# A new hand-over order and later, wider warm-up matmuls in an attention and feed-forward kernel

## The chip, the cores and the metric

The kernel runs on one core of a Trainium2 chip. Its five engines each take their instructions in order from a queue of their own: PE multiplies matrices, ACT and DVE work element by element, POOL and SP mostly issue transfers here. [...] The metric is device time in microseconds (us) of one execution; lower is better.

## The reference

Linear attention, whose result is the input of a two-layer network without biases and with an ELU between the layers.

```
q, k, v: (8, 8, 576, 64)                     # batch, head, row, channel; float32
q_s = exp(q - max) / sum over channels
k_s = exp(k - max) / sum over rows
kv  = einsum('bhsd,bhse->bhde', k_s, v)
att = einsum('bhsd,bhde->bhse', q_s, kv)
x   = att.transpose(0, 2, 1, 3).reshape(4608, 512)
h   = x @ w_in                               # (512, 2048)
g   = where(h > 0, h, exp(min(h, 0)) - 1)
out = g @ w_out                              # (2048, 512)
```

## The kernel before

The attention is cut into 16 units (one of 8 batches and four of its eight heads, all 576 rows). For a unit, ACT takes the exponential of the queries (tile QR) and keys (KR), DVE sums the queries (ZQ), inverts the sums and multiplies (QS); PE transposes QS (`tp`) into PSUM, ACT and DVE copy it to qsT; PE multiplies keys and values (`kv_mm`, 36 small matmuls), DVE scales the result into MBLK (`m`); PE multiplies qsT by MBLK (`ao_mm`) and ACT and DVE copy the rows to XT (`xt`). From the fifth unit on, the transpose is done by a transfer (`turn`, tile QT). The network runs over nine blocks of 512 rows: `hg_mm` makes 256 hidden columns at a time (eight matmuls of 512 columns with W1), the `hg` that follows turns them by exponential and comparison into GT on ACT and DVE, and `out_mm` multiplies GT by W2.

`Sched` records every operation with what it reads and writes. Nothing is scheduled at run time: the table ORDER lists, for each engine, the numbers of the operations in the order in which they are issued; numbers go by the order of `add`. The method `order` walks these lists with modelled durations to find a common sequence, `fill` adds warm-up matmuls on PE that compute nothing that is used, and `emit` puts in the semaphore waits. Numbers used below: 0 clears the identity ID; 1 (POOL) writes its diagonal; 25, 26, 27 are the sum, reciprocal and product of unit 0's queries, 37, 38, 39 those of unit 1; 30 and 28 are unit 0's transposes, 43 and 45 unit 1's; 32 and 50 are the key-value products; 47 and 54 the attention products; 49 and 46 are DVE's copies of XT (unit 0) and qsT (unit 1); 67 and 68 the first W1 matmuls.

The first loads (queries, keys, values of units 0 and 1) are issued by SP, in that order; POOL issues W1 once ID and the keys of unit 0 are there, then W2's four slices and the loads of units 2 and 3. The GT buffer of block 1 shares its memory with small buffers of the start, among them OSBX0 to OSBX3, from which the rows of block 0 are stored; DVE may write GT of block 1 there only after those stores have landed. In SP's list 161, 162 are the two stores of OSBX0, 164, 165 those of OSBX1, 167, 168 of OSBX2 and 170, 171 of OSBX3; 185 and 209 are transposes by transfer; 187, 190, 199, 200, 210, 216 are loads.

In `fill` of before, a run of warm-ups is put wherever PE is modelled idle for long enough, one for each 80 ns, 128 columns wide, and waits only for the identity:

```
idle = o.start - free - 150
count = int(idle / 80)
...
p.deps = {d: "raw" for d in self.spare_after}
```

Of the kernel before, what the change touches and what calls it, by code (L numbers as in the profile page):

```python
# [21 lines left out]
ISSUE = {"sp": 550, "act": 550, "gp": 740}  # L22
ORDER = {
    "pe": (
        "30 28 32 43 45 47 50 67 54 68 70 71 69 72 82 86 93 115 103 90 129 128 137 136 131 139 107 "
        "130 138 109 151 152 150 126 134 149 132 156 157 158 140 173 146 153 159 172 174 175 233 238 "
        "237 239 192 243 249 245 244 251 250 201 255 257 256 203 263 262 212 268 261 267 269 313 309 "
        "321 317 350 220 325 333 329 280 391 334 282 338 342 291 412 346 351 299 399 404 395 417 362 "
        "400 364 408 425 430 373 413 421 438 426 381 479 434 439 487 450 500 492 483 505 488 452 513 "
        "518 461 496 469 501 526 509 564 514 572 522 538 585 527 540 568 577 573 598 581 586 590 594 "  # L30
        "603 611 549 607 636 599 556 657 640 612 662 644 649 653 645 670 622 666 624 683 688 658 679 "
        "632 675 671 634 696 709 684 692 701 714 697 705 722 727 735 718 710 740 731 748 723 744 761 "
        "736 766 757 753 749 770 787 762 774 779 775 783 788 792 793 805 797 801 809 "),
    "act": (
        "3 22 33 23 24 31 29 34 35 48 44 55 73 76 77 79 83 84 87 94 95 97 104 91 92 116 117 119 98 "
        "108 120 127 135 133 163 160 179 147 166 154 169 205 176 230 231 188 234 180 240 241 191 246 "
        "215 252 253 202 258 204 211 264 213 265 273 270 214 218 310 322 314 217 284 318 221 279 326 "
        "294 355 281 330 296 335 283 290 392 343 297 292 339 293 347 366 352 376 300 405 361 396 378 "
        "363 401 409 365 372 418 375 443 414 454 379 422 374 431 427 382 464 435 449 480 440 451 466 "
        "493 467 484 531 489 453 460 463 506 519 462 497 470 502 542 510 515 565 537 523 539 554 551 "  # L40
        "528 569 578 574 541 552 616 582 591 587 595 548 555 550 608 637 600 626 557 604 641 613 650 "
        "654 621 646 623 663 667 689 631 625 659 680 633 676 672 685 693 715 702 698 635 706 719 728 "
        "711 732 741 724 745 737 767 758 750 771 754 763 776 780 784 789 794 798 806 802 810 812 "),
    "dve": (
        "2 4 5 0 6 7 25 26 37 27 38 39 40 41 42 36 46 49 51 52 53 56 74 75 78 80 81 85 88 89 96 100 "
        "105 106 101 102 122 118 110 111 112 123 124 141 142 143 148 155 182 183 184 177 178 232 206 "
        "235 236 193 194 207 195 196 197 242 208 247 198 248 254 259 260 266 274 275 271 272 276 311 "
        "312 285 319 222 223 286 320 224 225 226 227 287 327 328 356 331 332 357 336 337 358 344 345 "
        "348 349 367 353 368 354 301 369 302 303 304 305 306 397 398 402 403 410 411 444 415 416 445 "
        "446 423 424 428 429 383 384 455 385 386 387 388 436 456 457 437 441 442 485 490 486 532 491 "  # L50
        "498 499 533 471 503 472 534 473 474 504 511 543 544 512 475 476 516 517 524 525 545 529 530 "
        "570 571 575 576 583 584 596 597 617 588 618 589 609 610 601 558 602 619 642 643 559 627 560 "
        "561 562 614 615 628 629 563 655 656 647 648 668 669 660 661 673 674 681 682 686 687 694 695 "
        "707 699 708 700 720 721 712 713 733 734 725 726 746 747 738 739 759 760 751 752 772 764 765 "
        "773 777 778 785 786 "),
    "gp": (
        "1 14 15 16 17 18 19 20 21 57 59 58 63 60 61 62 64 66 99 65 113 125 144 121 114 145 181 186 "
        "189 "),
    "sp": (
        "8 9 10 11 12 13 170 187 161 164 171 185 165 190 200 168 162 199 209 210 216 167 219 277 278 "  # L60
        "229 228 323 315 288 295 316 289 324 298 341 359 308 360 377 307 340 393 370 371 406 394 420 "
        "380 407 419 447 433 390 465 482 432 458 448 389 494 481 495 459 468 478 507 520 535 477 567 "
        "508 521 536 553 566 546 580 547 579 620 605 638 606 593 592 630 651 652 639 677 665 690 664 "
        "678 703 716 717 691 730 704 729 756 768 769 742 755 743 782 781 790 791 795 796 799 800 807 "
        "808 803 804 811 "),
}


# [14 lines left out]
class Sched:  # L83
# [2 lines left out]
    ENG = ("pe", "act", "dve", "gp", "sp")  # L86
    OVER = {"pe": 163, "act": 105, "dve": 82, "gp": 110}
    LAND = 350
    SPIN_FROM = 9400.0
    FIRST = {"sp": 2050, "act": 2050, "gp": 2700}  # L90
    DMA_RATE = 385.0

# [67 lines left out]

    def fill(self, seq):

        out, free, done = [], self.SPIN_FROM, False
        for o in seq:
            if o.eng == "pe" and not done:
                idle = o.start - free - 150
                count = int(idle / 80)
                if count > 1 and all(d.end < free for d in self.spare_after):
                    p = Op("pe", count * 57, self.spare(count), 0)
                    p.start, p.end = free, free + p.dur  # L170
                    p.deps = {d: "raw" for d in self.spare_after}
                    out.append(p)
                free = o.end
                done = o is self.spare_until
            out.append(o)
        return out

    def emit(self, seq):
# [61 lines left out]
class Gen:  # L240
# [394 lines left out]
    def program(self):  # L635
# [28 lines left out]
        for o in S.ops:  # L664
# [1 line left out]
                o.late = False  # L666
        S.spare_after = [self.ident]
        S.spare = lambda count: lambda e: [e.matmul(
            self.PS[0][:, 0:128], self.ID[:, :], self.ID[:, :], start=True, stop=True)
            for _ in range(count)][-1]  # L670

        self.load_w2(0, -29)
# [87 lines left out]
        key = 0  # L760
# [101 lines left out]
```

The softmax here doesn't subtract the row's maximum and nothing guards it: scores larger than these inputs give would overflow.

## Time and profile before

| | us |
|---|---|
| median of 4 runs | 300.98 (300.61 to 301.87) |
| profiled execution, its own time | 300.78 |
| its span, first to last instruction | 299.0 |
| PE busy | 286.7 |
| DVE busy | 189.5 |
| ACT busy | 182.0 |

The span is what the profile's rows lie in; the execution's time has 1.8 us around it. PE's matmuls are pipelined and the end of each is modelled, so the pace of a group is better read from its start to the start of the next group than from its duration. A bracket at the end of a timeline row gives the engine's idle time before it and what ended that. Engine PEld is PE's loading of weights, which runs beside its matmuls. In the rows of windows the columns are the stretch, its length, then busy time and count of PE, PEld, DVE, ACT and POOL, the granted clock, the share of the transfer engines and their GB/s.

### The profile page before, as it was taken

The page shows a single profiled execution, that of the slowest core. Times are in us where ns is not written, and L with a number is a line of the kernel's source. Part 1 is how long each engine was busy: PE and PEld are TensorE (multiplying, and loading weights), DVE is VectorE, ACT ScalarE, POOL GpSimd, SP SyncE. Part 2 cuts the span into 40 slices and gives each one's busy share as a digit, 9 for nine tenths or more (in the row PEclk, how much of TensorE's full clock was granted, in tenths as well). Part 3 has the DMA queues.
Part 4 walks back from the last instruction along what each step waited for, and adds up shares of the span by engine and source line. Part 5 has one row for each costly group of instructions (what it writes and reads, how often), then busy time and mean ns, then how long its engine had stood idle before and what let it go on. Part 6 is the DMA issues. An engine that isn't in the chain of part 4 may idle for free.

```text
span 299.0 us, 4448 instructions
## 1 busy us (share of the span) xinstructions
PE 286.7 (96%) x1865; PEld 236.1 (79%) x1865; DVE 189.5 (63%) x244; ACT 182.0 (61%) x212; POOL 21.7 (7%) x33
## 2 busy tenths in 40 slices
PE   1699999999999999999999999999999999999995
PEld 1578877687888888888888888888888888888885
DVE  3958935985898685894568855588427256655500
ACT  5768848998977967867755766534462423432411
POOL 0860244100000000000000000000000000000000
PEclk9999999999999999999999999999999999999999
DMA  7999998995497896389546226041312302004214
GB/s 262 395 396 391 389 389 262 280 285 198 120 277 227 125 350 187 73 261 275 166 116 165 89 78 172 2 100 37 85 37 50 72 0 53 0 0 107 64 41 105
DMA packets 35443, 49.96 MB, mean 167 GB/s; under 512 B 16352, under 2 KB 16608, under 8 KB 35424
## 3 DMA queue, kind: packets, MB, share of 16 engines
q1 hardware_dynamic: 29840, 34.15, 41.7%
q0 software_dynamic: 5504, 15.47, 16.2%
q8 instruction: 14, 0.23, 0.3%
q10 hardware_dynamic: 80, 0.07, 0.1%
q14 instruction: 5, 0.04, 0.0%
HBM read 36.70 MB, written 9.44 MB: 154 GB/s over the span
## 4 chain that ended last, share of the span: by engine, by line
PE 92%; DMA 4%; ACT 1%; DVE 0%; SPq 0%; POOL 0%; issue 0%
PE PS L588 44%; PE PS L543 43%; PE PS L487 3%; DMA KR<-in_k_dram 2%; DMA W<-in_moe_w_in_dram 2%; PE PS L456 2%; ACT ESB L559 1%; DVE GT L572 0%; ACT ESB L570 0%; PE PS L403 0%; SPq L315 0%; POOL W L332 0%; ACT OSB L598 0%
## 5 line engine op out<-in xcount | busy, mean ns | idle before, releaser
L588 PE MATMUL PS<-W,GT 128*128 128x512 f32 (+1 forms) x592 | 141.4, 386 | 0.4 <-DVE GT L578 0.4
L543 PE MATMUL PS<-XT,W 128*128 128x512 f32 x576 | 140.3, 391 | 0.2
L543 PEld LDWEIGHTS PS<-XT,W 128*128 128x128 f32 x576 | 107.2, 188 | 23.2 <-DVE XT L512 0.5
L588 PEld LDWEIGHTS PS<-W,GT 128*128 128x128 f32 x592 | 107.7, 188 | 22.1 <-DVE GT L578 0.8
L559 ACT ACTIVATE ESB<-PS 128x1024 f32<-128x1024 f32 x72 | 73.8, 1027 | 65.5 <-PE PS L543 65.3
L576 DVE TENSOR_SCALAR ESB<-ESB 128x1024 f32<-128x1024 f32 x64 | 44.2, 692 | 66.6 <-ACT ESB L559 65.9
L578 DVE TENSOR_TENSOR GT<-ESB,PS 128x1024 fp32r<-128x1024 f32 x64 | 77.7, 1217 | 1.8
L620 ACT ACTIVATE OSB<-PS 128x512 f32<-128x512 f32 x31 | 18.2, 597 | 30.6 <-PE PS L588 30.6
L372 DVE TENSOR_REDUCE ZQ<-QR 128x18 f32<-128x1152 f32 x16 | 21.5, 1343 | 7.3 <-ACT QR L352 7.2
L509 ACT ACTIVATE XT<-PS 128x512 fp32r<-128x512 f32 (+6 forms) x32 | 19.5, 609 | 8.1 <-PE PS L487 7.6
L380 DVE TENSOR_TENSOR QS<-QR,RZQ 128x1152 f16<-128x1152 f32 x16 | 21.6, 1353 | 0.3
L352 ACT ACTIVATE QR<-QR 128x1152 f32<-128x1152 f32 x16 | 18.6, 1165 | 2.8 <-DMA QR<-in_q_dram 2.8
L356 ACT ACTIVATE KR<-KR 128x1152 bf16<-128x1152 f32 x16 | 18.4, 1160 | 2.3 <-DMA KR<-in_k_dram 2.3
L487 PE MATMUL PS<-qsT,MBLK 128*128 128x320 f32 (+5 forms) x64 | 14.4, 311 | 0.0
L487 PEld LDWEIGHTS PS<-qsT,MBLK 128*128 128x128 f32 x64 | 12.0, 194 | 2.6 <-DVE MBLK L469 0.2
L431 ACT ACTIVATE qsT<-QT 128x1152 fp32r<-128x1152 f16 x12 | 13.9, 1162 | 0.0
L365 ACT ACTIVATE VB<-VR 128x1152 bf16<-128x1152 f32 (+1 forms) x12 | 13.5, 1125 | 0.7 <-DMA VR<-in_v_dram 0.7
L572 DVE SCALAR_TENSOR_TENSOR GT<-PS,ESB 128x1024 fp32r<-128x1024 f32 x8 | 9.8, 1221 | 4.5 <-ACT ESB L570 4.4
L403 PE MATMUL PS<-ID,QS 128*128 128x128 f16 x36 | 3.7, 266 | 6.8 <-DVE QS L380 6.8
L469 DVE TENSOR_TENSOR MBLK<-PS,RZK 64x128 fp32r<-64x128 f32 x32 | 9.2, 288 | 0.9
L403 PEld LDWEIGHTS PS<-ID,QS 128*128 128x128 f16 x36 | 2.9, 122 | 7.4 <-DVE QS L380 7.0
L570 ACT ACTIVATE ESB<-ESB 128x1024 f32<-128x1024 f32 x8 | 8.5, 1060 | 0.2
(29 smaller groups left out, 60.0 us busy)
## 6 DMA issues: line engine op xcount, KB each, us to landing
out_dram<-OSB SPq DMA_DIRECT2D x62, 128.0 KB, 2.4
QR<-in_q_dram SPq DMA_DIRECT2D x12, 576.0 KB, 4.7
KR<-in_k_dram SPq DMA_DIRECT2D x12, 576.0 KB, 5.9
VR<-in_v_dram SPq DMA_DIRECT2D x12, 576.0 KB, 5.4
W<-in_moe_w_out_dram POOLq DMA_DIRECT2D x4, 1024.0 KB, 18.2
QR<-in_q_dram POOLq DMA_DIRECT2D x4, 576.0 KB, 11.1
KR<-in_k_dram POOLq DMA_DIRECT2D x4, 576.0 KB, 11.2
VR<-in_v_dram POOLq DMA_DIRECT2D x4, 576.0 KB, 8.1
```

The costliest lines, as they stand in the source:

```text
L352: S.add("act", t_act(1152, False), lambda e: e.activation(flat(q), flat(q), AF.Exp), key - 3, X=[f"qR{i}"], follow=self.table)
L356: S.add("act", t_act(1152, False), lambda e: e.activation(ek[:, :, :, :].rearrange("p h c d -> p (h c d)"), flat(k), AF.Exp), key - 2, X=[ ...
L372: S.add("dve", t_dve(1152), lambda e: e.tensor_reduce(self.ZQ[i][:, :, :].rearrange("p h c -> p (h c)"), q[:, :, :, :].rearrange("p h c d ...
L380: S.add("dve", t_dve(1152), lambda e: e.tensor_tensor(qso, q[:, :, :, :], rz, ALU.mult), key - 3, R=[f"qR{i}", f"RZQ{i}"], W=[f"QS{self.al ...
L487: last = e.matmul(P[:, y:y + n_], M[:, f, :], T[:, c0:c1, f * 64:f * 64 + 64], start=True, stop=True)
L509: S.add("act", t_act((h1 - h0) * n_, True), lambda e, dst=dst, src=src: e.activation(dst, src, AF.Copy), key, W=W, X=X)
L543: last = e.matmul(P[:, t * 512:(t + 1) * 512], self.W1[:, kc, tt * 128:(tt + 1) * 128], self.XT[:, kc, rc:rc + BLK], start=(kc == 0), stop ...
L559: S.add("act", t_act(1024, True), lambda e: e.activation(esb[:, :], P[:, :], AF.Exp), key, W=[f"E{i}"], X=banks)
L576: S.add("dve", t_dve(1024, 2), lambda e: e.tensor_scalar(esb[:, :], esb[:, :], 1.0, -1.0, ALU.min, ALU.add), key, X=[f"E{i}"])
L578: S.add("dve", t_dve(1024), lambda e: e.tensor_tensor(gt, esb[:, :], P[:, :], ALU.max), key, R=[f"E{i}"], W=gw, X=banks)
L588: last = e.matmul(dst, GT[:, jj, ts * 128:(ts + 1) * 128], self.W2[:, jj, c0:c1], start=(jj == 0), stop=(jj == 15))
L620: S.add("act", t_act(512, True), lambda e: e.activation(osb[:, :], src, AF.Copy), key, W=[f"O{i}0", f"O{i}1"], X=[f"b{bk}"])
```

## The change

Three things are changed. All five lists of ORDER are new. In `fill`, a run of warm-ups may start from 7.9 us of the modelled time on, waits also for the last ACT or DVE operation that is modelled to end before it, and is counted with 430 ns for one in the first run and 260 ns in the later ones; the test that the identity is modelled ready is gone. A warm-up is now 512 columns wide: the identity repeated four times as the moving operand. The built program has runs of 3, 3 and 5 warm-ups in place of 12, 3 and 6: 3 ahead of operation 30, 3 ahead of 32 and 5 ahead of 47.

```diff
 ORDER = {
     "pe": (
-        "30 28 32 43 45 47 50 67 54 68 70 71 69 72 82 86 93 115 103 90 129 128 137 136 131 139 107 "
-        "130 138 109 151 152 150 126 134 149 132 156 157 158 140 173 146 153 159 172 174 175 233 238 "
-        "237 239 192 243 249 245 244 251 250 201 255 257 256 203 263 262 212 268 261 267 269 313 309 "
+        "30 28 32 47 43 45 50 68 54 67 70 71 69 72 82 86 93 103 90 115 129 128 107 137 136 130 109 "
+        "131 138 150 126 139 152 132 159 157 149 156 134 140 151 146 153 173 175 158 172 174 233 239 "
+        "237 192 243 238 244 245 251 250 249 256 201 257 203 255 263 262 212 261 267 268 269 313 321 "
...
     "act": (
-        "3 22 33 23 24 31 29 34 35 48 44 55 73 76 77 79 83 84 87 94 95 97 104 91 92 116 117 119 98 "
+        "3 22 33 23 24 29 34 31 35 48 44 55 73 76 77 79 83 84 87 97 94 95 104 91 98 92 116 108 119 "
...
     "dve": (
-        "2 4 5 0 6 7 25 26 37 27 38 39 40 41 42 36 46 49 51 52 53 56 74 75 78 80 81 85 88 89 96 100 "
+        "4 5 2 6 7 25 26 0 27 37 38 39 40 41 42 36 49 46 51 52 53 56 74 75 78 80 81 85 88 89 100 96 "
...
     "gp": (
-        "1 14 15 16 17 18 19 20 21 57 59 58 63 60 61 62 64 66 99 65 113 125 144 121 114 145 181 186 "
+        "1 14 15 16 17 18 19 20 21 59 57 60 58 61 63 62 66 64 65 113 99 125 114 121 144 145 181 186 "
         "189 "),
     "sp": (
-        "8 9 10 11 12 13 170 187 161 164 171 185 165 190 200 168 162 199 209 210 216 167 219 277 278 "
+        "8 9 10 11 12 13 185 187 164 162 190 167 161 200 199 171 209 216 165 168 210 170 277 229 278 "
...
-    SPIN_FROM = 9400.0
+    SPIN_FROM = 7900.0
...
     def fill(self, seq):
 
-        out, free, done = [], self.SPIN_FROM, False
+        free, done, spares = self.SPIN_FROM, False, []
+        timed = [o for o in seq if o.eng in ("act", "dve") and not o.dma]
         for o in seq:
             if o.eng == "pe" and not done:
-                idle = o.start - free - 150
-                count = int(idle / 80)
-                if count > 1 and all(d.end < free for d in self.spare_after):
-                    p = Op("pe", count * 57, self.spare(count), 0)
+                count = int((o.start - free - 150) / (430 if free == self.SPIN_FROM else 260))
+                if count > 0:
+                    p = Op("pe", count * 220, self.spare(count), 0)
                     p.start, p.end = free, free + p.dur
                     p.deps = {d: "raw" for d in self.spare_after}
-                    out.append(p)
+                    near = [d for d in timed if d.end + self.hop(d, p) <= free]
+                    p.deps[max(near, key=lambda d: d.end)] = "raw"
+                    spares.append((o, p))
                 free = o.end
                 done = o is self.spare_until
-            out.append(o)
+        out = []
+        for o in seq:
+            out += [p for q, p in spares if q is o] + [o]
         return out
...
         S.spare = lambda count: lambda e: [e.matmul(
-            self.PS[0][:, 0:128], self.ID[:, :], self.ID[:, :], start=True, stop=True)
+            self.PS[0][:, 0:512], self.ID[:, :], self.ID[:, :].unsqueeze(1).broadcast_to([128, 4, 128]),
+            start=True, stop=True)
             for _ in range(count)][-1]
```

## The prediction

> **What bounds the kernel now.** I read the page's busy shares and chain of waits, then the first 18 us of the timeline, then PE's gaps in the body, then SP's queue.
>
> ```profile
> PE 286.7 (96%) x1865; PEld 236.1 (79%) x1865; DVE 189.5 (63%) x244; ACT 182.0 (61%) x212; POOL 21.7 (7%) x33
> PE 92%; DMA 4%; ACT 1%; DVE 0%; SPq 0%; POOL 0%; issue 0%
> ```
>
> PE is the bound: its matmuls make 92% of the chain that ends last, so any gap in PE after the stream has begun lengthens the run by itself. Before that, the head counts. The timeline (start, duration):
>
> ```profile
> 1.54 0.28 POOL L293 TENSOR_SCALAR_AFFINE_SELECT ID<-ID 128x128 f16<-128x128 f16 x1 [1.10 <-DVE VB L302]
> ...
> 1.88 1.46 PE L668 MATMUL PS<-ID 128*128 128x128 f16 x12 [1.88 <-POOL ID L293]
> ...
> 7.30 0.27 DVE L376 RECIPROCAL RZQ<-ZQ 128x18 f32<-128x18 f32 x1
> 7.48 1.29 DVE L372 TENSOR_REDUCE ZQ<-QR 128x18 f32<-128x1152 f32 x1
> ...
> 8.69 1.34 DVE L380 TENSOR_TENSOR QS<-QR,RZQ 128x1152 f16<-128x1152 f32 x1
> ...
> 10.09 1.14 PE L403 MATMUL PS<-ID,QS 128*128 128x128 f16 x9 [6.75 <-DVE QS L380]
> ...
> 11.17 0.71 PE L456 MATMUL PS<-VB,KR 64*64 64x65 bf16 x36
> ...
> 13.03 1.20 PE L487 MATMUL PS<-qsT,MBLK 128*128 128x512 f32 x2
> ...
> 14.03 0.63 PE L668 MATMUL PS<-ID 128*128 128x128 f16 x6
> 14.59 0.48 PE L456 MATMUL PS<-VB,KR 64*64 64x65 bf16 x36
> 15.21 1.17 PE L543 MATMUL PS<-XT,W 128*128 128x512 f32 x4
> ```
>
> The twelve old warm-up matmuls run at 1.88, then PE idles 6.75 us. The granted-clock column says 1.00 everywhere, but the pace does not: nine transposes take 1.07 us from their start at 10.09 to the next group's (0.119 each), and 0.49 us at 36.39; 36 key-value products (L456) take 0.71 us at 11.17 and 0.48 at 14.59. So PE runs at about half speed until a point between 14.03 and 14.59, 3.9 to 4.5 us after it became steadily busy. The first feed-forward matmuls stand at 15.21 just behind the first W1 slices, whose transfer ends at 15.12 in the chain:
>
> ```profile
> 9.20 5.92 DMA W<-in_moe_w_in_dram
> ```
>
> **The change, part by part.** The sum is made on the profiled execution, 300.78 us with a span of 299.0. The median is 300.98, 0.20 above it.
>
> *Identity.* In DVE's new order the memset of ID stands behind unit 0's sum and reciprocal (7.30 + 0.27 = 7.57), no longer at the start. Before, PE began 0.6 us after that memset ended (1.19 + 0.11 = 1.30, then 1.88), so the first new warm-up starts at about 8.2. It names an ACT operation, unit 1's query exponential (ended at 7.38), but that is not what it waits for longest. Behind it in PE's queue stand unit 0's transposes. W1's first transfer waits for ID too, and for unit 0's keys (8.16 before): cost nothing, covered by the six loads ahead of it in the transfer engines; uncovered, some 0.1 us.
>
> *Unit 0's query product.* It moves ahead of unit 1's sum on DVE (7.48, 1.29), so it ends near 9.0, not 10.03.
>
> *Warm-ups, 3 + 3 + 5 of 512 columns.* At half speed one costs four 128-wide ones: 12 took 1.46 with the tail of the last, so 0.105 to 0.119 each, 0.42 to 0.48; I take 0.42. At full speed 0.227 (60 in 13.7). PE then runs: 8.2, three to 9.47 (transposes were ready at 9.1); transposes 1.07 to 10.54; three to 11.81; key-value product 0.65 (11.16 to 11.81 before) to 12.46. If the clock again takes 3.9 to 4.5 us from the start of steady work, it is full at 12.1 to 12.7. Five warm-ups at full speed end at 13.6. The attention product (L487) could have started at about 13.1, when ACT's second copy of qsT, now behind unit 1's key exponential, is done; the warm-ups hold it 0.5 us.
>
> *XT and the first bank.* L487 at full speed reaches its copy in 0.65 us (16.22 to 16.88), so at 14.25. DVE now does the XT copy before unit 1's qsT copy (both 0.69), and PE's first W1 matmuls go to the bank that the second copy frees: 14.25 + 1.40 + 0.07 = 15.7, against 15.21. Then eight matmuls and unit 1's product, ten at 0.227, reach the second W1 half at 17.97 against 17.62: +0.3. Ends: -0.1 if the clock is early (15.21 + 2.27 = 17.48; W1's landing forbids more); +1.9 if it is never full before (five at 0.42 to 14.56, L487's 1.25 to its copy, 1.47, 2.27: 19.5).
>
> [...]
>
> *The new order in the body.* The largest gaps of PE:
>
> ```profile
> 50.05 4.70 PE L543 MATMUL PS<-XT,W 128*128 128x512 f32 x20
> ...
> 55.13 1.21 PE L588 MATMUL PS<-W,GT 128*128 128x512 f32 x4 [0.38 <-DVE GT L578]
> ...
> 56.42 2.11 PE L543 MATMUL PS<-XT,W 128*128 128x512 f32 x8
> ```
> ```profile
> 52.00:56.00 4.00, 3.62 (x17) 2.61 (x15) 3.77 (x4) 3.90 (x4) 1.15 (x1) 1.00 0.87 253
> 56.00:60.00 4.00, 3.93 (x86) 2.79 (x85) 3.93 (x7) 3.53 (x5) 0.00 (x0) 1.00 1.13 284
> ```
>
> From start to next start: 5.08 - 20 x 0.227 = 0.54; 1.28 - 4 x 0.227 = 0.37; 58.45 - 56.42 - 8 x 0.227 = 0.21: together 1.1 us. All wait for DVE (third busy column, 3.77 and 3.93 of 4 us) to turn block 1's activations. The new PE order puts eight W1 matmuls (1.81 us, operation 239) ahead of the products that wait (237, 238). That can hide all of it, -1.1; but DVE has the same operations to do and is full, so the wait may come back in the next ones, 0. I take half, -0.55.
>
> *SP's queue.* Stores of block 0's rows (OSBX) share memory with block 1's GT, so DVE's L578 at 69.54 waits for the OSBX0 and OSBX1 stores. Their last one was issued near 60.2. In the new order it is operation 165, moved past a load pair, the second QT transpose and a load.
>
> ```profile
> 63.32 1.83 SPq L419 DMA_TRANSPOSE QT<-QS  x1
> 65.20 0.58 SPq L315 DMA_DIRECT2D QR<-in_q_dram  x1
> ...
> 66.33 0.49 SPq L630 DMA_DIRECT2D out_dram<-OSBX  x1
> ```
>
> So it issues near 63 + 1.83 + 0.58 = 65.4. The store that stood behind those (66.33) took 5.8 us to land, so 71.2, up to 1.7 us after 69.54. DVE's next consumer on PE is a bank for the L543 at 72.27, 1.5 us after that L578 ended (70.76): that slack is the cover. I take +0.2; ends 0 and +1.7. The other loads move inside transfers that land ahead of their use before (the 576 KB loads in 4.7 to 5.9 us): nothing, and 1 us if one does not. On POOL's queue one load more now stands ahead of W2's first and second slice, 1.5 us (576 KB at some 390 GB/s). The second landed at 14.92 + 16.0 = 30.9 and is first used by the third group of L588 matmuls, at 30.82 + 1.9 = 32.7, in the new order behind transposes (0.49): 32.4 against 33.2, nothing; without those 0.8 us of cover it costs what is over.
>
> *Sum:* +0.3 - 0.55 + 0.2 = -0.05 on the profiled execution, 300.7; the median 0.2 above as now: **300.9**.
>
> **Rivals.**
> 1. *The warm-ups become the path* (slower). Eleven of them at half speed are 4.6 us of PE work ahead of real work, in a head where PE has none to spare: if the clock is not full until the stream begins, +1.9 in place of +0.3: 302.5. It decides once the release is later than about 14.2. For it: release came no sooner than 3.9 us after work began. Against: PE is steadily busy 1.9 us earlier. It is also how the change would fail its own words.
> 2. *Stores late.* If the L578 slack is gone, +1.7 in place of +0.2: 302.4. For it: stores issued at 59.7 and 60.3 took 6.2 us; against: the second transpose comes a little earlier in the new order.
> 3. *All of it works.* Clock early (-0.1), all 1.1 hidden, stores covered: 300.98 - 1.2 = 299.8. Against: DVE's 94 to 98% in that stretch.
>
> **How the numbers follow.** The forecast has 0.56, the rivals 0.17, 0.10 and 0.17. A measurement here tells 0.3%, 0.9 us, from no change: below 300.08 or above 301.88. Rival 3 and a sliver of the forecast make faster, 0.18; three quarters of rival 1, most of rival 2 and a little of the forecast make slower, 0.22; the rest is 0.60. The forecast's own range is 300.2 to 301.6 (body from -1.1 to 0, head 0 to 0.7). The range for 8 in 10 reaches into rivals 1 and 2, and to rival 3's figure: 299.9 to 302.3.
>
> **What would show it.** Right: warm-ups start near 8.2 behind POOL's ID; the key-value products of unit 1 take 0.48 us; the second W1 half starts between 17.5 and 18.3; PE's gaps between 52 and 59 shrink to about half. Wrong: L487 at half pace and a W1 stream beginning after 16.5 (rival 1); DVE's GT at 69 to 71 released by a store (rival 2); a PE gap at a place not named here, most likely a W2 slice near 32 to 38 or a load between 83 and 107, would be a step that I have missed.

## The result, and the profile after

The changed kernel takes 302.51 us (median of 40 runs, 301.31 to 303.89) where the kernel before, run beside it, takes 301.13 (65 runs, 300.38 to 302.84): ratio 1.0041, 95% interval 1.0033 to 1.0049. By the ratio it is slower by 1.2 us, beyond the 0.3% that the text set as its bound and above the forecast's range. The profiled execution took 302.26 us, with a span of 300.5.

The page's busy shares and its chain, engine by engine, of the changed kernel:

```profile
PE 287.8 (96%) x1855; PEld 234.8 (78%) x1855; DVE 189.4 (63%) x244; ACT 181.1 (60%) x212; POOL 22.9 (8%) x33
PE 95%; DMA 1%; DVE 1%; ACT 1%; POOL 0%; issue 0%; POOLq 0%
```

PE is the bound as before, and now the chain's transfers have shrunk from 4% to 1%: the start of the stream no longer stands behind W1's landing. The timeline of the first 20 us (start, duration) shows behind what it stands:

```profile
7.51 0.11 DVE L296 MEMSET ID<- 128x64 uint32 x1
7.58 1.36 DVE L384 TENSOR_TENSOR QS<-QR,RZQ 128x1152 f16<-128x1152 f32 x1
7.87 1.23 POOL L297 TENSOR_SCALAR_AFFINE_SELECT ID<-ID 128x128 f16<-128x128 f16 x1 [7.42 <-DVE ID L296]
...
9.15 1.46 PE L672 MATMUL PS<-ID 128*128 128x512 f16 x3 [9.15 <-POOL ID L297]
9.40 5.09 POOL L336 DMA_DIRECT2D W<-in_moe_w_in_dram  x8 [0.31 <-POOL ID L297]
...
10.41 1.17 PE L407 MATMUL PS<-ID,QS 128*128 128x128 f16 x9
...
12.79 0.71 PE L460 MATMUL PS<-VB,KR 64*64 64x65 bf16 x36
...
13.43 1.76 PE L672 MATMUL PS<-ID 128*128 128x512 f16 x5
...
14.84 0.81 PE L491 MATMUL PS<-qsT,MBLK 128*128 128x512 f32 x2
...
15.68 0.69 DVE L516 CAST XT<-PS 128x512 fp32r<-128x512 f32 x1 [0.53 <-PE PS L491]
...
16.29 0.68 DVE L417 CAST qsT<-PS 128x512 fp32r<-128x512 f16 x1
...
17.02 1.20 PE L547 MATMUL PS<-XT,W 128*128 128x512 f32 x4 [0.45 <-DVE qsT L417]
...
19.46 2.59 PEld L547 LDWEIGHTS PS<-XT,W 128*128 128x128 f32 x12 [0.29 <-DVE XT L516]
```

POOL's select that writes the identity, 0.28 us before, runs 1.23 us here, from 7.87 to 9.10; DVE's product of unit 0's queries runs beside it and ends at 8.94. The first warm-up waits for it until 9.15. Everything that PE does then comes late: the attention product (L491) at 14.84, not 13.03, the first W1 matmuls at 17.02, not 15.21, and the second W1 half at 19.46 (its weight load; 17.63 before): 1.83 us lost in the head. W1 is issued 0.94 us later too (9.40, 8.46 before), and the fourth of its eight transfers, which the second half needs, lands at 19.17 by the trace's record of landings (17.06 before), 0.29 us ahead of the group that uses it. The profile shows no wait of PE for it, but the margin is small.

From there on the changed kernel is a little shorter. The stretch up to the W1 group near 72 us takes 54.30 us (73.77 less 19.46, before rounding), against 54.65 before (72.27 less 17.62), and from that group to PE's last matmul both take 223.4. So +1.83 - 0.35 = +1.48, the difference of the profiled executions (302.26 - 300.78). The windows that showed DVE's hold on PE before:

```profile
52.00:56.00 4.00, 4.00 (x20) 3.25 (x19) 3.08 (x4) 3.60 (x5) 0.00 (x0) 1.00 0.94 292
56.00:60.00 4.00, 4.00 (x88) 3.14 (x86) 3.88 (x5) 4.00 (x5) 1.33 (x1) 1.00 0.85 164
```

PE (first busy column) is full in both, where it had 3.62 and 3.93.

### The profile page after: what moved, and what is told of

Read it like the earlier page. It is cut to its first block, busy times and chain, and to the rows that moved or that the text cites. A ratio compares the mean times of both kernels' runs of the same rounds, so it can differ in the third digit from the quotient of the medians.

```text
span 300.5 us, 4425 instructions
## 1 busy us (share of the span) xinstructions
PE 287.8 (96%) x1855; PEld 234.8 (78%) x1855; DVE 189.4 (63%) x244; ACT 181.1 (60%) x212; POOL 22.9 (8%) x33
## 4 chain that ended last, share of the span: by engine, by line
PE 95%; DMA 1%; DVE 1%; ACT 1%; POOL 0%; issue 0%; POOLq 0%
PE PS L547 44%; PE PS L592 44%; PE PS L491 3%; PE PS L460 2%; PE PS L672 1%; DMA QR<-in_q_dram 1%; PE PS L407 1%; DVE ZQ L376 0%; POOL ID L297 0%; ACT QR L356 0%; DVE XT L516 0%; DVE qsT L417 0%; ACT OSB L602 0%; DVE RZQ L380 0%; DVE ID L296 0%
## 5 line engine op out<-in xcount | busy, mean ns | idle before, releaser
L563 ACT ACTIVATE ESB<-PS 128x1024 f32<-128x1024 f32 x72 | 73.8, 1027 | 66.2 <-PE PS L547 66.0
L491 PE MATMUL PS<-qsT,MBLK 128*128 128x320 f32 (+5 forms) x64 | 14.0, 305 | 0.0
L491 PEld LDWEIGHTS PS<-qsT,MBLK 128*128 128x128 f32 x64 | 11.7, 190 | 2.8 <-DVE MBLK L473 0.2
L672 PE MATMUL PS<-ID 128*128 128x512 f16 x11 | 4.7, 571 | 9.2 <-POOL ID L297 9.2
L672 PEld LDWEIGHTS PS<-ID 128*128 128x128 f16 x11 | 1.2, 132 | 10.5 <-POOL ID L297 9.1
```

The source lines that it names most:

```text
L491: last = e.matmul(P[:, y:y + n_], M[:, f, :], T[:, c0:c1, f * 64:f * 64 + 64], start=True, stop=True)
L563: S.add("act", t_act(1024, True), lambda e: e.activation(esb[:, :], P[:, :], AF.Exp), key, W=[f"E{i}"], X=banks)
```

## The experiments

Ratios are to the kernel before, run on the same chip beside each. The table's times are starts in the profiled executions (us); "stretch" runs from the second W1 half to the W1 group near 72; "clock" is when the trace records the granted rate going to full (its columns show 1.00 for the time ahead of the first record).

| | ratio | interval | first warm-up | L491 | second W1 half | stretch | clock |
|---|---|---|---|---|---|---|---|
| before | 1 | | 1.88 | 13.03 | 17.63 | 54.65 | 14.28 |
| changed | 1.0041 | 1.0033-1.0049 | 9.15 | 14.84 | 19.46 | 54.30 | 14.50 |
| e1 | 0.9976 | 0.9964-0.9988 | 1.88 | 13.07 | 18.02 | 54.81 | 15.52 |
| e2 | 1.0035 | 1.0022-1.0049 | 9.13 | 14.39 | 19.19 | 55.43 | not recorded |
| e3 | 0.9984 | 0.9971-0.9997 | 7.34 | 13.53 | 18.16 | 54.31 | 13.39 |
| e4 | 1.0056 | 1.0035-1.0076 | none | 13.07 | 20.01 | 54.94 | 19.47 |
| e5 | 0.9987 | 0.9973-1.0002 | 1.58 | 12.76 | 17.38 | 54.53 | 5.66 |
| e6 | 0.9977 | 0.9964-0.9990 | 1.58 | 13.20 | 17.52 | 54.99 | 5.05 |
| e7 | 0.9995 | 0.9980-1.0010 | 7.45 | 12.98 | 17.38 | 55.08 | 12.80 |
| e8 | one run | | 9.57 | 14.84 | 19.37 | 54.45 | 13.67 |
| e9 | 0.9981 | 0.9965-0.9997 | 1.58 | 12.97 | 17.29 | 54.36 | 5.19 |
| e10 | 0.9984 | 0.9966-1.0001 | 1.88 | 12.34 | 17.27 | 54.26 | 6.09 |
| e11 | 1.0039 | 1.0023-1.0056 | 9.06 | 14.60 | 19.36 | 54.29 | 14.11 |
| e12 | 1.0101 | 1.0073-1.0129 | (10.37, transposes) | 13.28 | 20.51 | 56.20 | 13.94 |

The first two part head and body.

**e1, old head and new body**

```diff
 "pe":  up to 86 as before, from 93 as changed
 "act": up to 55 as before, from 73 as changed
 "dve": up to 56 as before, from 74 as changed
 "gp", "sp": as changed;  warm-ups: as before
```

> The kernel before, with its own first operations and warm-ups (PE up to operation 93, ACT up to 73, DVE up to 74), and behind them the changed kernel's order on every engine, with its POOL and SP lists. Theory H (the loss is made in the head): the second half of W1's first matmuls starts at 17.6 as before (19.46 in the changed kernel), and the time is 0.3 us below before, ratio 0.999, since from that point to PE's last group the changed trace is 0.33 us shorter. Theory B (the new order of the body, its loads or stores cost): ratio 1.003 or more.

**e2, new head and old body**: the same cut, the other way round, with the changed warm-ups.

> The changed kernel with the order of before behind the head (PE from operation 93, ACT from 73, DVE from 74, POOL and SP lists of before). Theory H: the second half of W1's first matmuls starts near 19.4, and the time is 1.2 to 1.8 us above before, ratio 1.004 to 1.006, so no better than the changed kernel. Theory B: ratio 1.000 to 1.001.

e1 comes out at 0.9976, e2 at 1.0035: the loss goes with the head, and behind the old head the new order of the rest is a gain. Theory B falls. Two things do not fit as well. The profiled execution of e1, the slowest of its twelve (301.37), shows no gain in the stretch (54.81). And behind the new head no gain of the body can be told: 1.0041 with the new body, 1.0035 with the old one, with intervals that overlap. In e2 PE's weight loads also waited for W1 slices, 1.1 us in two places: W1 was issued at 9.39 there, as late as in the changed kernel, and the fourth transfer landed at 18.95.

**e3, the identity first**

```diff
-        "4 5 2 6 7 25 26 0 27 37 38 39 ...
+        "4 0 5 2 6 7 25 26 27 37 38 39 ...
```

> The changed kernel with one operation moved: DVE clears the identity among its first memsets again, not behind unit 0's sum. Theory I (the late identity, with POOL's select stretched to 1.23 us beside DVE's multiply, makes most of the head's loss): POOL's select takes 0.28 us near 1.5, the warm-ups begin at 7.5 and not at 9.15, W1's issue at 8.5 and not at 9.4, the second W1 half starts 1.0 to 1.7 us sooner than 19.46, and the ratio to before falls from 1.004 to 1.000 to 1.001. Theory W (the eleven warm-ups at half speed, or the copy order behind them, make it): the second W1 half starts less than 0.5 us sooner, ratio 1.003.

The timeline of e3:

```profile
1.24 0.28 POOL L297 TENSOR_SCALAR_AFFINE_SELECT ID<-ID 128x128 f16<-128x128 f16 x1 [0.79 <-DVE ID L296]
...
7.34 1.46 PE L672 MATMUL PS<-ID 128*128 128x512 f16 x3 [7.34 <-ACT QR L356]
...
8.30 5.09 POOL L336 DMA_DIRECT2D W<-in_moe_w_in_dram  x8 [6.78 <-DMA KR<-in_k_dram]
8.92 1.14 PE L407 MATMUL PS<-ID,QS 128*128 128x128 f16 x9
...
13.53 0.82 PE L491 MATMUL PS<-qsT,MBLK 128*128 128x512 f32 x2
...
15.72 1.20 PE L547 MATMUL PS<-XT,W 128*128 128x512 f32 x4 [0.45 <-DVE qsT L417]
```

One moved memset turns 1.0041 into 0.9984, about 1.7 us by the medians of the two comparisons and 1.30 us at the second W1 half. Only now do the warm-ups wait for the ACT operation that they name. Theory I holds; W, as a first cause, falls. e3 takes away three things at once: the late place of the memset, the stretched select behind it, and the late issue of W1 (8.30 here; the fourth transfer lands at 16.74). No run takes away the stretch alone.

**e4, no warm-ups**

```diff
-        return self.fill(sorted(seq, key=lambda o: (o.start, rank[o])))
+        return sorted(seq, key=lambda o: (o.start, rank[o]))
```

> The changed kernel without any warm-up; order and waits else the same. Theory W (warm-ups lie on the path): the key-value product of unit 0 starts near 11.0 and not 12.8, the attention product near 13.2 and not 14.84, and the second W1 half starts 0.5 to 1.5 us sooner unless the clock stays at half speed past 16; ratio 1.001 to 1.003. Theory I (the warm-ups cost nothing but begin too late to help): the clock comes later and the ratio is 1.004 or more.

The timeline of e4, around PE's attention products and its first W1 matmuls:

```profile
13.07 1.19 PE L491 MATMUL PS<-qsT,MBLK 128*128 128x512 f32 x2 [1.51 <-ACT qsT L414]
...
16.04 2.08 PE L547 MATMUL PS<-XT,W 128*128 128x512 f32 x4
17.91 1.05 PE L491 MATMUL PS<-qsT,MBLK 128*128 128x512 f32 x2
```

Both theories had a part right. The attention product comes 1.8 us earlier without the warm-ups, so they do lie on the path; but four W1 matmuls then take 1.87 us to the next group, 0.47 each, and the clock is full only at 19.47. The ratio, 1.0056, lies 0.15% above the changed kernel's 1.0041, but the intervals overlap: whether such late warm-ups gain anything can't be told.

**e5, 16 warm-ups from the start** (on top of e3)

```diff
+                first = free == self.SPIN_FROM
+                if first:
+                    count = 16
...
-                    near = [d for d in timed if d.end + self.hop(d, p) <= free]
-                    p.deps[max(near, key=lambda d: d.end)] = "raw"
+                    if not first:
+                        near = [d for d in timed if d.end + self.hop(d, p) <= free]
+                        p.deps[max(near, key=lambda d: d.end)] = "raw"
```

> The kernel with the identity cleared first, and the first run of warm-ups made 16 instead of 3, waiting only for the identity, so that PE is busy from 1.6 on. Theory C (what is left of the head's loss is the clock, which is released only after a whole window of 3.41 us of steady PE work): the clock is full before 8.8 us, warm-ups and unit 0's products all run at full pace, the second W1 half starts at 17.5 to 17.9 (18.16 with the identity first alone), runs scatter less, and the time falls by a further 0.3 to 0.7 us, ratio to before 0.996 to 0.997. Theory K (what is left is the order of DVE's copies and the first bank): second W1 half not before 18.0, ratio 0.998 as without.

**e6, and the old first bank**

```diff
-        "30 28 32 47 43 45 50 68 54 67 70 ...
+        "30 28 32 47 43 45 50 67 54 68 70 ...
```

> As the run with 16 early warm-ups, and PE's first W1 matmuls go to the bank of before (operation 67 ahead of 68), which waits for the XT copy alone and not for the copy of unit 1's transposes behind it. Theory K: the W1 stream starts 0.5 us sooner, down to the landing of W1 at 15.1, and the second half with it; ratio 0.994 to 0.996. Theory C: with the clock full early both copies are done before W1 has landed, so no difference within 0.1 us.

The 3.41 us of theory C is the step in which the trace's record of the clock changes (half speed for 3.41 us in e12, below). The clock was full at 5.66 (e5) and 5.05 (e6), 4.08 and 3.47 us after the first warm-up; in none of these runs did it come sooner after steady work than in e6. With it full that early, the second W1 half starts at 17.38, so the clock was the rest of the head's loss, and a little more; the bank adds nothing (17.52), as theory C said. The first W1 matmuls start at 14.96 (e5) and 14.88 (e6), when the slices that they need have landed at 14.71 and 14.83, so little is left to gain there. But the times did not follow: the ratios (0.9987 and 0.9977) can't be told from e3's 0.9984, the runs of e5 scatter from 300.05 to 301.76, and the stretch has grown (54.53 and 54.99, 54.31 in e3). The timeline of e6 near 72 us shows a part of it:

```profile
71.14 1.22 DVE L586 TENSOR_TENSOR GT<-ESB,PS 128x1024 fp32r<-128x1024 f32 x1 [1.97 <-DMA out_dram<-OSBX]
...
72.51 1.86 PE L551 MATMUL PS<-XT,W 128*128 128x512 f32 x7 [0.43 <-DVE GT L586]
```

DVE waits 1.97 us for a store, and PE 0.43 us behind it: the store that the prediction's second rival named. In the changed kernel's timeline DVE waits too (in brackets: the wait ahead and what ended it), PE does not:

```profile
72.24 1.22 DVE L582 TENSOR_TENSOR GT<-ESB,PS 128x1024 fp32r<-128x1024 f32 x1 [1.20 <-DMA out_dram<-OSBX]
...
74.48 1.23 DVE L576 SCALAR_TENSOR_TENSOR GT<-PS,ESB 128x1024 fp32r<-128x1024 f32 x1 [1.02 <-ACT ESB L574]
```

The same store holds DVE in e1, e3, e4, e5 and e8 too, 1.2 to 2.1 us. PE waits behind it in e1 (0.41 us) and e8 (0.31), and not in e3 and e5. An early head does not decide it: the head of e8 is late, those of e3 and e5 are early.

**e7, the new warm-ups in the old order** (5 ahead of the transposes, then 1 and 1)

```diff
 class Sched, S.spare: as changed
 ORDER: as before
```

> The order table of before on all engines, with the changed warm-ups: 5 of 512 columns ahead of the first transposes, waiting for an ACT or DVE operation, then 1 and 1. The identity is early here. Theory I (the loss came from the identity's new place in the order): the warm-ups start near 9.0, the clock comes up to 1 us sooner than before, ratio 0.998 to 1.000. Theory W (wide warm-ups at half speed cost in themselves): unit 0's transposes start at 11 and not 10.1, ratio 1.002 or more.

The warm-ups began at 7.45, not near 9.0. The ratio is 0.9995, with an interval around 1: with the identity early, wide and later warm-ups cost nothing and bring nothing that the interval can tell. The clock came 1.5 us sooner than in the old profile (12.80), the second W1 half 0.25 us sooner, and the stretch was 0.43 us longer in this one execution.

**e8, the identity one place later**

```diff
-        "4 5 2 6 7 25 26 0 27 37 ...
+        "4 5 2 6 7 25 26 27 0 37 ...
```

> The changed kernel with the memset of the identity one place later, behind unit 0's query product, so that POOL's select falls under DVE's sum over one operand and not under its product of two. The run of warm-ups ahead of the transposes becomes 4, the next 1. Theory P (DVE's product of two operands holds POOL off): the select takes 0.28 us again, 9.2 to 9.5. Rival (any DVE work beside it stretches it, or the identity's memset just before it): about 1.2 us again. One look, no verdict on time.

The timeline of e8, where the memset stands just ahead of DVE's sum:

```profile
8.88 0.11 DVE L296 MEMSET ID<- 128x64 uint32 x1
8.90 1.29 DVE L376 TENSOR_REDUCE ZQ<-QR 128x18 f32<-128x1152 f32 x1
...
9.23 0.28 POOL L297 TENSOR_SCALAR_AFFINE_SELECT ID<-ID 128x128 f16<-128x128 f16 x1 [8.78 <-DVE ID L296]
```

The select, cleared and released in the same way, takes 0.28 us beside DVE's sum over one operand: theory P. It is DVE's product that holds it (1.23 us in the changed kernel), not the memset ahead nor any work of DVE beside it. The product differs from the sum in reading two operands and in writing 1152 columns, not 18; these runs do not part the two.

**e9, e10, e11, the stores first**

```diff
-        "... 200 199 171 209 216 165 168 210 170 277
+        "... 200 199 171 165 168 209 216 170 210 277
```

in the kernel of e6 (e9), in the early warm-ups with the old head (e10), and in the changed kernel itself (e11).

> The kernel with the identity first, 16 early warm-ups and the old first bank, and in SP's list the last stores of OSBX1 and OSBX2 (165, 168) ahead of the second transposing transfer and the load behind it, that of OSBX3 (170) ahead of the next load. Theory S (the stores that the new order moved back hold DVE's GT and through it PE, 0.4 us, once the head is early): DVE's wait for OSBX near 71 (2.0 and 0.9 us) and PE's wait of 0.43 us there go, from the second W1 half to the 32 later groups at 72 us takes 54.3 us instead of 55.0, ratio to before 0.995 to 0.9965. Rival L (the loads now land later and hold another engine instead): the stretch stays at 54.8 to 55.2, ratio 0.9975 to 0.999.

> As the run with the stores first, but with the order of before up to the first feed-forward groups (so unit 1's sum again ahead of unit 0's product) and warm-ups of 16, 1 and 1. If the head ends at W1's landing in either order, as theory C has it, the second W1 half starts at 17.4 to 17.6 here too and the ratio equals that of the other within 0.001. If the head's new order is worth something by itself, this is 0.2 us or more slower.

> The changed kernel with nothing but the same move in SP's list. Theory H with covered stores: DVE's wait for OSBX (1.20 us at 72) goes, PE's start at 73.8 does not move by more than 0.1 us since nothing on PE waited for it, ratio to before 1.003 to 1.005. Theory S for this kernel too: 0.3 us less, ratio 1.001 to 1.003.

No wait of DVE on a store is left in any of the three. In e9 the stretch falls from 54.99 to 54.36 and PE's wait near 72 is gone, as theory S said; the ratio, 0.9981, is outside what S said (0.995 to 0.9965) and can't be told from e6's. In e11 PE's group near 73.8 starts at 73.65, the stretch is unchanged (54.29) and the ratio is 1.0039, with 1.0041 for the changed kernel: there the late store was covered, theory H. e10's head ends at 17.27, as e9's does at 17.29, and the ratios are 0.9984 and 0.9981: with the clock full early, these runs show no difference between the two orders of the head.

**e12, the late identity in the old order**

```diff
-        "2 4 5 0 6 7 25 26 37 27 38 39 ...
+        "2 4 5 6 7 25 26 37 0 27 38 39 ...
```

> The kernel before with one operation moved: DVE clears the identity only behind both sums, just ahead of unit 0's product, so POOL's select falls beside that product and the first run of 12 warm-ups is no longer placed. Theory Q (the late identity costs by way of W1 too): the select ends with the product near 10.1, W1 is issued at 10.3 and not 8.46, PE waits for W1 slices between 15 and 24, 0.5 to 1.5 us in all, and the ratio is 1.002 to 1.005. Rival (W1's issue is covered by the six loads ahead of it, as the prediction had it): the transposes start near 10.1 as before, the second W1 half near 17.6, ratio 0.999 to 1.001.

The timeline of e12, with the select, W1's issue and the matmuls of its second half:

```profile
9.11 1.12 POOL L293 TENSOR_SCALAR_AFFINE_SELECT ID<-ID 128x128 f16<-128x128 f16 x1 [8.66 <-DVE ID L292]
...
10.53 5.09 POOL L332 DMA_DIRECT2D W<-in_moe_w_in_dram  x8 [0.31 <-POOL ID L293]
...
20.51 9.80 PE L543 MATMUL PS<-XT,W 128*128 128x512 f32 x35 [2.00 <-DMA W<-in_moe_w_in_dram]
```

Theory Q, and more than it: W1 is issued at 10.53, PE stands 2.00 us for its second half, and just behind that hole, at 20.77, the clock falls back. The window of 20 to 24 us of e12 shows it; the last three columns are the granted clock (0.60), the DMA share and GB/s:

```profile
20.00:24.00 4.00, 3.49 (x9) 2.77 (x10) 0.58 (x1) 1.02 (x1) 2.23 (x3) 0.60 1.19 413
```

The ratio is 1.0101. The prediction's "cover" of W1's issue, six loads ahead of it, is thus thin. In the eight kernels that issue W1 between 8.05 and 8.52, the fourth transfer lands between 16.40 and 17.06; in the five that issue it between 9.27 and 9.82 (the changed kernel, e2, e4, e8 and e11), between 18.85 and 19.17; in e12 at 20.26. In these traces an issue 0.9 us later thus lands about 2 us later. Why that is more than the delay of the issue, no run shows.

## Why the prediction was wrong, point by point

**Identity: the step that failed.** The text put the first warm-up at 8.2: the memset's end plus 0.6 us, taken from a row in which DVE was clearing small tiles. The price of POOL's select between the two was thus the 0.28 us of that row. The place of the memset in DVE's queue was read rightly (7.51 to 7.62); the duration of POOL's operation behind it was not. Beside DVE's product the select takes 1.23 us, so 9.15, 0.95 us late. e3, without the late select, comes out at 0.9984, and e8 shows that the product is the reason. The select took 1.23 us (changed) and 1.12 us (e12) beside the product of two operands, 0.28 beside the sum over one (e8); by what means the product holds it, no run shows. That W1 waits for the identity too was said and priced at nothing. That fails with the same step: issued at 9.40, the fourth transfer lands at 19.17, so the second W1 half could not have begun at the forecast's 17.97 even with PE on time. PE shows no wait for W1 only because the rest of the head was as late; e12 shows the wait. How the 1.83 us divide between the late warm-ups and W1 stays open.

**Warm-ups and clock: sized too small.** The text let the clock be full at 12.1 to 12.7, from one release 3.9 to 4.5 us after steady work. It was 14.50, 5.35 us after 9.15, so the last five warm-ups took 1.41 us and not 1.13, and L491 started 14.84, not 13.6. One row of one kernel was too little to go by: in the runs the release came from 3.5 us (e6: 1.58 to 5.05) to 6.4 us (e4: 13.07 to 19.47) after steady work. The 0.7 us at the upper end of the forecast's head was the author's estimate and no run shows it; the head came out at +1.83, with the release at 14.50.

**XT and the first bank.** The mechanism was right (PE's first W1 matmuls wait 0.45 us for the qsT copy), 17.02 against a forecast of 15.7 only for what came before it. Together the head cost 1.83 us where +0.3 was forecast.

**The body.** -0.55 was forecast, -0.35 seen in the stretch. Behind the old head the ratio of e1 agrees in sign (0.9976, about 0.7 us); behind the new one, e2 does not tell. The gaps of 1.1 us between 52 and 59 are gone; as the stretch is only 0.35 us shorter, some 0.75 us came back elsewhere in it, as the text allowed.

**SP's queue.** The late store was foreseen, with its place; DVE waited 1.20 us for it, where up to 1.7 was forecast. So the sign of the second rival came true without its price: the cost on PE was 0, an end of the range, not the +0.2 chosen (e11). In the executions of e1, e6 and e8 PE did wait, 0.31 to 0.43 us.

**The rivals.** The first came nearest: +1.9 in the head, decided by a release later than 14.2. The release was at 14.50, so that condition was met, but the clock was full 2.5 us before the stream began (17.02), not only with it. The number fits (+1.83) in part by luck: of the 1.83 us the identity's lateness, with the select and W1's issue behind it, makes 1.30 (e3), and what is left of the clock's lateness the rest (e5). The identity's delay was not in this rival.

**The median.** The text added the 0.2 us by which the old median lay above the profiled execution. That held: 302.51 against 302.26 here. What makes a kernel's runs scatter stays open. That it is the clock's varying release is not shown: e9, whose profiled execution has the clock full at 5.19, scatters from 299.89 to 301.64 all the same.

**What beats both kernels.** e1, e3, e6 and e9 lie 0.2% below before with intervals that exclude 1; which of them is best can't be told from these runs. The changed kernel with the identity's memset at the front (e3) is the smallest such edit of it.

## What to carry to other kernels

Price a moved operation with its new neighbours: a row gives its duration beside what ran then, and POOL's select, which gates two queues, took 0.28 us in the row and 1.23 us beside another engine's work. When an order table is solved anew, look first at the cheap set-up operations that have slid backwards, and at every queue that waits for them: here the warm-ups and W1's transfers. In these runs the clock was full 3.5 us (e6) to 6.4 us (e4) after PE's steady work began, so work that is to warm it should begin that far ahead of the work it is for, with nothing late in front of it; counted to fill a modelled hole, it became part of the path here (L491 at 14.84, without it at 13.07).

## What the runs showed of the hardware

- POOL's select of 128x128 beside DVE's two-operand product of 1152 columns took 1.23 and 1.12 us (changed, e12) and ended 0.16 us after the product in both; beside DVE's sum over one operand (e8), or beside memsets (before, e3), 0.28 us.
- The record of the clock holds a state for whole multiples of 3.413 us from its first entry on: in before and in the changed kernel full speed for 286.72 (84 of them), in e12 full speed for 6.83, half for 3.41, then full for 279.89 (2, 1 and 82). The stretches below are counted from a change in steps of 3.413 us: an estimate from these records.
- In e12 PE stood 2.00 us (18.51 to 20.51), and the record has the clock at half from 20.77 to 24.18. The length of the gap does not decide it: in e5 1.88 us of idleness (7.20 to 9.08) at the end of the first 3.41 us after the release (5.66 to 9.07), and in e6 2.48 us (6.90 to 9.38), across the end of such a stretch at 8.46, did not lower it: nine transposes behind the gap took 0.51 us to the next group in both. What decides it, no run shows.
- In e4 the last stretch of 3.41 us but one before the release, 12.64 to 16.05, had PE at work from 13.07 on, and the clock was not released at its end; the next, 16.05 to 19.47, was filled from end to end, and at its end the clock was full.
- The fourth of W1's transfers landed at 16.40 to 17.06 when W1 was issued by 8.52, at 18.85 to 19.17 when it was issued at 9.27 to 9.82, and at 20.26 when it was issued at 10.53 (e12).
